# Attention with memory, leaky MLP and bilinear MLP on one core: the first batch's scores with tokens on partitions, the first chunk of w_out loaded by column halves, the last product in two column parts

## The chip, the cores and the metric

The kernel runs as one launch on one core of a Trainium2 chip. The metric is the device time of the launch in microseconds; the kernel before was timed three times. TensorE (PE) multiplies, VectorE (DVE) and ScalarE (ACT) convert, reduce and copy, SyncE (SP) issues every transfer, GpSimd (POOL) does almost nothing here. Each engine carries out its instructions strictly in the order in which they stand in the program.

## The reference

Three stages follow one another, all in float32 (the weights come as float64 words, which the kernel converts itself):

```python
a = exp(phi - max(phi, over m));  a = a / (sum(a, over m) + 1e-9)     # B=4, H=8, S=576, M=32
k_m = einsum('bhsm,bhsd->bhmd', a, k);  v_m = same with v             # D=64
s = q @ k_m^T / 8;  s = exp(s - max);  attn = s / (sum(s) + 1e-9)
x = (attn @ v_m) laid out as 2304 tokens x 512
h = x @ w_in                      # 512 -> 2048
y = maximum(0.01*h, h) @ w_out    # 2048 -> 512
out = ((y @ w_a) * (y @ w_b)) @ w_out2     # 512 -> 1536 -> 512
```

## The kernel before

**Stages.** For each batch `b` a head (`kv_part`, line 547; `sc_both`, line 653) loads phi, k and v, takes the exponentials of phi (ACT, line 537), turns them on PE (`ta`, `tz`, lines 584 and 587), copies them to SBUF (`en`, line 407), multiplies them with k and v (`km`, line 603: 20 float32 matmuls of two passes each), scales (`kvn`, line 613), turns the result (`kvt`, line 623) and copies it out as `kd` (keys) and `vm` (values). Scores (`sc`, line 667) come with the 32 memory slots on partitions and tokens along the row, 320 or 256 columns; DVE turns them in squares of 32 (line 688), and max, subtraction, ACT's exponential (line 699), sum, reciprocal and product (lines 697 to 707) run on 128 partitions; a second turn (line 711) gives `at`.

**The first MLP.** `w_in` and `w_out` are taken in four chunks `c` of 512 hidden columns, each in four pieces of 512 KB (`weight`, line 451). A piece is two ACT passes (`high` and `low`, lines 470 and 473) and four DVE passes (clamp, shift, join, add; lines 477 to 488); `w_out` is then split into two fp32r parts (a cast, line 407, and a subtraction, line 494). `vw` (line 750) multiplies `vm` into `w_in`, so that `h` (lines 803 and 821) is attention times `vw`. Batch 0 of chunk 0 uses plain float32 (`vwf`, `gf`, lines 803, 774 and 867); everything else three fp32r passes. Tokens go in eight pieces `n`: piece `x` = 0 of batch 0 has 320 columns, `x` = 1 has 256. Each of the four `h` of a piece is read by ACT (line 774), mostly twice: once to `g`, once to `t`.

**The second MLP.** Products with `w_a` and `w_b` by seven instead of eight sub-products (line 1092 and 1146), then `o` (line 1186), an add on DVE (line 1199), and two output transfers per 512 columns (line 1205).

**Order.** A planner (`Program`, lines 113 to 333) sets the order once, when the program is built. Each operation has a cost on the engines that may do it, a due time `late` (worked back from the main products' times, less a `slack`), and tiles that must find a free buffer in a room. At each moment every engine takes the ready operation that is due first. PSUM has eight banks: room "h" is three of them (for `h`), "y" two, "x" three (for `ta`, `tz`, `km`, `kvt`, `sc`, `vw`). SP's transfers are planned the same way and land one after another. After some tiles of the head, `idle` (line 430) puts four PE transpositions that compute nothing (line 434), and `warm` (line 424) puts 38 of them at the start.

Of the kernel before, what the change touches and what calls it, by code (L numbers as in the profile page):

```python
# [53 lines left out]
FULL = (0,)  # L54
TURN = 0.15
FILL = 4
WARM = 38
SEVEN = 8
LEAD = 37
SLACK = {'phi0': 72.94, ('kv0', 0): -15.48, ('kv0', 1): -17.72, 'kvr0': -10.62, ('q0', 0): 4.66, ('q0', 1): 32.32, ('win0', 0): 0.75, ('win0', 1): 103.86, ('wout0', 0): 20.54, ('wout0', 1): -39.84, 'win': -23.08, 'wout': 22.71, 'wa': -4.25, 'wb': -26.57, 'wout2': -2.14, ('sc', 0, 0): 57.16, ('sc', 0, 1): -2.31, ('sc', 1, 0): 13.24, ('sc', 1, 1): 6.37, ('sc', 2, 0): 23.27, ('sc', 2, 1): 24.61, ('vw', 0, 0): 85.06, ('vw', 0, 1): -56.75, ('vw', 0, 2): 18.69, ('vw', 1, 0): 5.23, ('vw', 1, 1): 100.39, ('vw', 1, 2): 9.67}  # L60
START = 15.05
BIAS = 0.52
POOL_BIAS = 9.26
LAT, LAT_SAME, LAT_DMA = 0.503, 0.134, 3.8
OVER = {'DMA': 0.0, 'PE': 0.0, 'ACT': 0.1, 'DVE': 0.019, 'POOL': 0.0}
BLOCKED = 2.31
DMA_RATE = 355000.0
SPARE = {'DMA': 1.27, 'PE': 1.0, 'ACT': 1.03, 'DVE': 1.03, 'POOL': 0.96}

# [38 lines left out]
class Program:  # L108
# [13 lines left out]
    def op(self, eng, cost, fn, r=(), w=(), tiles=(), pos=None, ahead=60.0, keep=0, slack=0.0, soon=False):  # L122
# [213 lines left out]
def tile_mem_attention__leaky_mlp__bilinear_mlp(  # L336
# [93 lines left out]
    def idle(tile, get, token):  # L430
# [20 lines left out]
    def weight(kind, c, k, after=()):  # L451
# [73 lines left out]
    def phi_stats(b, gs, phi, st):  # L525

        nmx, es, er = ([(n, b % 2, g) for g in gs] for n in ("nmx", "es", "er"))
        part = slice(gs[0], gs[-1] + 1)
        e = [("e", b, g) for g in gs]
        op(  # L530
            "DVE", c_dve(S * len(gs)), lambda T: nc.vector.tensor_reduce(st[0][:, part], T[phi], axis=AX.X, op=ALU.max, negate=True),
            r=e, w=nmx, tiles=[phi],
        )
# [12 lines left out]

    def kv_part(b, g):
# [49 lines left out]

        def k_m(T):
            for t in range(5):
                n = P if t < 4 else 64  # L600
                src = T[kvt[t // 2]][:, t % 2, :] if t < 4 else T[rest][:, g, :]
                for h in range(4):
                    nc.tensor.matmul(  # L603
                        T[km][h * M:(h + 1) * M, :], T[en][0:n, t, h * M:(h + 1) * M], src[:, h * P:(h + 1) * P],
                        start=(t == 0), stop=(t == 4),
                    )

        op("PE", 1.5, k_m, r=[(en, 0), (en, 1), *kvt, rest], w=[km], tiles=[en, *kvt, rest, km])

# [31 lines left out]
    def q_load(b, g):
# [5 lines left out]
        for x in range(2):  # L647
# [3 lines left out]
            op("DMA", c_dma(P * n * 8), lambda T, q=q, cols=cols: nc.sync.dma_start(T[q], qT[b, g, :, :, cols]), w=[q], tiles=[q], slack=SLACK["q0", x])  # L651

    def sc_both(b, x):

        cols = piece(2 * b + x)
        n = cols.stop - cols.start
# [14 lines left out]

        op("PE", 4 * n / 2.4e3 + TURN, s_sc, r=[*qs, *(("kd", b % 2, g) for g in range(2))], w=scs, tiles=[*qs, *scs])
        NM = n // 32
# [58 lines left out]
    def vw_unit(c, b, x, n):  # L732
# [12 lines left out]
        def prod(T):  # L745
# [6 lines left out]
        op(  # L752
            "PE", TURN + 4 * n / 2.4e3, prod, r=[("a", k[1:]) for k in ws] + [("vm", b, g) for g in range(2)], w=os, tiles=[*os, *ws],
            ahead=15.0,
        )
        slack = SLACK["vw", min(c, 1), b - b % 2 if c else min(b, 2)]
        for i, o in enumerate(os):
            if whole(c, b):
                op(copy_by(n, True), 0, lambda T, e, i=i, o=o: copy(e, T[fk][:, i, cols], T[o]), r=[o], w=[(fk, i, x)], tiles=[o, fk], slack=slack)
                if b == 0:  # L760
                    idle(fk, lambda t, i=i: t[:, i, x * n:x * n + P], (fk, i, x))
                continue
# [27 lines left out]
    def h_unit(c, n, f, pos):  # L790
# [5 lines left out]
        if whole(c, b):  # L796
# [48 lines left out]
    def y_unit(c, k, e, pos, part=None):  # L845
# [12 lines left out]
        gs = [g_of(c, k, f) for f in range(4)]  # L858
        ws = [("wout", c, f) for f in range(4)]
        n, fine = ns[0], whole(c, ns[0] // 2)  # L860
        if fine:
            gf, cvs = ("gf", n), [("cv", "wout", c, f) for f in range(4)]

        def prod(T):
            for f, (g, j) in enumerate(gs):
                if fine:
                    nc.tensor.matmul(T[o], T[cvs[f]][:, 0, es].bitcast(F32), T[gf][:, f, :], start=f == 0, stop=f == 3)  # L867
                    continue
                w = T["wout", c, f]
# [297 lines left out]

    def o_unit(s, c, l, e, pos):


        size = NB2 if l < 2 else B * LEFT
        o = ("o", s, c, l, e)
        ps_ = [(("p", s, x, l), 0) if l < 2 else (("pl", c // 2), x % 2) for x in (c, c + 1)]
        ws = [("wout2", x, s) for x in (c, c + 1)]
# [4 lines left out]
        else:  # L1179
            tile_of(acc, "slot", [2, size] if l < 2 else [4, size])  # L1180
        es = slice(e * P, (e + 1) * P)

        def prod(T):
            for x, ((g, at), w) in enumerate(zip(ps_, ws)):
                for k, (u, v) in enumerate(PASSES):
                    nc.tensor.matmul(  # L1186
                        T[o], T[w][:, u, es], T[g][:, at, v, :], start=(x == 0 and k == 0), stop=(x == 1 and k == 2)
                    )
# [8 lines left out]
        else:  # L1197
            op(
                "DVE", c_dve(size), lambda T: nc.vector.tensor_tensor(T[acc][:, i, :], T[o], T[acc][:, i, :], op=ALU.add),  # L1199
                r=[o], w=[ka], tiles=[o, acc],  # L1200
            )
        if c == NC2 - 2:
            for at, w, to in places_of(s, l):
                op(
                    "DMA", c_dma(P * w * 4), lambda T, at=at, w=w, to=to: nc.sync.dma_start(out[:, e, to:to + w], T[acc][:, i, at:at + w]),
                    r=[ka], tiles=[acc], ahead=1e12,
                )
# [136 lines left out]
    for c in range(NC1):  # L1344
# [101 lines left out]
```

## Time and profile before

| | |
|---|---|
| three runs | 788.04, 787.47, 786.38 us; median 787.47 |
| profiled execution | 786.36 us, of which the span is 784.6 us |
| PE busy | 773.4 us (99%) |
| weight loads (PEld) | 663.4 us (85%) |
| DVE busy | 607.2 us (77%) |
| ACT busy | 379.1 us (48%) |
| DMA | 149.99 MB, mean 191 GB/s |

Busy shares are means over the span. The page's 40 slices give PE 7 and 8 tenths in the first two, 9 tenths in all but the last; the granted TensorE clock is at 9 tenths or more in every slice.

### The profile page before, as it was taken

The page shows a single profiled execution, that of the slowest core. Times are in us where ns is not written, and L with a number is a line of the kernel's source. Part 1 is how long each engine was busy: PE and PEld are TensorE (multiplying, and loading weights), DVE is VectorE, ACT ScalarE, POOL GpSimd, SP SyncE. Part 2 cuts the span into 40 slices and gives each one's busy share as a digit, 9 for nine tenths or more (in the row PEclk, how much of TensorE's full clock was granted, in tenths as well). Part 3 has the DMA queues.
Part 4 walks back from the last instruction along what each step waited for, and adds up shares of the span by engine and source line. Part 5 has one row for each costly group of instructions (what it writes and reads, how often), then busy time and mean ns, then how long its engine had stood idle before and what let it go on. Part 6 is the DMA issues. An engine that isn't in the chain of part 4 may idle for free.

```text
span 784.6 us, 12658 instructions
## 1 busy us (share of the span) xinstructions
PE 773.4 (99%) x4822; PEld 663.4 (85%) x4822; DVE 607.2 (77%) x1149; ACT 379.1 (48%) x817; POOL 0.7 (0%) x6
## 2 busy tenths in 40 slices
PE   7899999999999999999999999999999999999997
PEld 6567898989898988998888888888888888888886
DVE  5888988868888865686745899998995667898865
ACT  5767777747465635453445454445332254223210
POOL 0000000000000000000000000000000000000000
PEclk9999999999999999999999999999999999999999
DMA  9993331573247300035867547475488586978503
GB/s 321 384 323 140 99 90 61 192 264 103 82 174 266 124 1 1 1 115 206 293 247 267 185 160 273 161 239 190 164 322 346 178 275 209 354 250 280 179 19 108
DMA packets 56557, 149.99 MB, mean 191 GB/s; under 512 B 7216, under 2 KB 22576, under 8 KB 56496
## 3 DMA queue, kind: packets, MB, share of 16 engines
q1 hardware_dynamic: 56496, 149.18, 54.5%
q8 instruction: 38, 0.62, 0.3%
q14 instruction: 23, 0.19, 0.1%
HBM read 103.55 MB, written 45.61 MB: 190 GB/s over the span
## 4 chain that ended last, share of the span: by engine, by line
PE 95%; DMA 2%; DVE 1%; SPq 0%; ACT 0%; issue 0%
PE y L871 24%; PE abx L1092 17%; PE o L1186 13%; PE h L821 13%; PE abz L1092 8%; PE os L1301 5%; PE aby L1092 4%; PE b L1146 2%; PE a L1146 2%; PE y L867 2%; PE vw L750 2%; DMA kv<-in_kv_dram 1%; DMA phi<-in_phiT_dram 1%; PE h L803 1%; PE km L603 1%; PE sc L667 0%
## 5 line engine op out<-in xcount | busy, mean ns | idle before, releaser
L871 PE MATMUL y<-g,wout 128*128 128x320 f32 (+2 forms) x1104 | 197.2, 333 | 0.0
L871 PEld LDWEIGHTS y<-g,wout 128*128 128x128 f32 x1104 | 175.6, 188 | 16.7 <-issue 2.1
L1092 PE MATMUL abx<-yb_T,wo 128*128 128x512 f32 x432 | 109.7, 389 | 0.0
L1103 ACT COPY t<-abx 128x512 f32<-128x512 f32 x72 | 42.3, 587 | 122.7 <-PE abx L1092 117.6
L1092 PEld LDWEIGHTS abx<-yb_T,wo 128*128 128x128 f32 x432 | 80.6, 188 | 16.4
L1186 PE MATMUL o<-p,wout 128*128 128x512 f32 x384 | 93.6, 389 | 0.0
L1186 PEld LDWEIGHTS o<-p,wout 128*128 128x128 f32 x384 | 71.9, 188 | 15.2 <-DVE osum L1199 0.4
L774 ACT ACTIVATE g<-h 128x256 fp32r<-128x256 f32 (+1 forms) x120 | 49.7, 414 | 52.9 <-PE h L821 50.8
L821 PE MATMUL h<-ahi,vwh 128*128 128x256 f32 (+1 forms) x240 | 72.7, 303 | 0.0
L821 PE MATMUL h<-ahi,vwl 128*128 128x256 f32 (+1 forms) x240 | 71.0, 296 | 0.0
L821 PE MATMUL h<-alo,vwh 128*128 128x256 f32 (+1 forms) x240 | 71.0, 296 | 0.0
L890 DVE TENSOR_TENSOR acc<-y,acc 128x320 f32<-128x320 f32 (+1 forms) x72 | 40.1, 557 | 36.6 <-PE y L871 35.7
L837 DVE TENSOR_TENSOR g<-t,g 128x256 fp32r<-128x256 f32 (+1 forms) x120 | 53.7, 453 | 15.4 <-ACT t L774 14.4
L821 PEld LDWEIGHTS h<-ahi,vwh 128*128 128x128 f32 x240 | 45.4, 189 | 10.2 <-issue 3.6
L774 ACT ACTIVATE t<-h 128x256 f32<-128x256 f32 (+1 forms) x120 | 49.5, 413 | 0.0
L821 PEld LDWEIGHTS h<-alo,vwh 128*128 128x128 f32 x240 | 45.4, 189 | 0.2
L821 PEld LDWEIGHTS h<-ahi,vwl 128*128 128x128 f32 x240 | 45.5, 190 | 0.0
L1100 DVE TENSOR_TENSOR t<-abz,t 128x512 f32<-128x512 f32 x48 | 33.0, 688 | 13.2 <-PE abz L1092 7.6
L1199 DVE TENSOR_TENSOR oacc<-o,oacc 128x512 f32<-128x512 f32 x40 | 27.6, 690 | 16.7 <-PE o L1186 16.2
L1092 PE MATMUL abx<-yb_B,wo 128*128 128x512 f32 x144 | 36.9, 391 | 0.0
L1092 PE MATMUL aby<-yb_B,wo 128*128 128x512 f32 x144 | 36.7, 390 | 0.0
L407 ACT CAST p<-t 128x512 fp32r<-128x512 f32 x32 | 19.9, 621 | 34.7 <-DVE t L1124 22.7
(289 smaller groups left out, 1276.1 us busy)
## 6 DMA issues: line engine op xcount, KB each, us to landing
k_wo<-wo SPq DMA_DIRECT2D x32, 512.0 KB, 4.4
wo<-k_wo SPq DMA_DIRECT2D x32, 512.0 KB, 4.9
raw_wout<-in_w_out_dram SPq DMA_DIRECT2D x24, 512.0 KB, 5.5
raw_win<-in_w_in_dram SPq DMA_DIRECT2D x16, 512.0 KB, 5.2
kv<-in_kv_dram SPq DMA_DIRECT2D x16, 512.0 KB, 10.4
k_yb_T<-yb_T SPq DMA_DIRECT2D x8, 512.0 KB, 5.9
raw_wa<-in_w_a_dram SPq DMA_DIRECT2D x8, 512.0 KB, 4.5
raw_wb<-in_w_b_dram SPq DMA_DIRECT2D x8, 512.0 KB, 5.4
```

The lines of the kernel that those rows point to most:

```text
L774: nc.scalar.activation(dst, src, AF.Prelu, alpha=0.01)
L821: nc.tensor.matmul(T[o], T[w[u]][:, k, fs], T[a[v]][:, k, cols], start=(k == 0 and i == 0), stop=(k == 1 and i == 2))
L837: lambda T, e: engines[e].tensor_tensor(T[g][:, i, 1, to], T[t], T[g][:, i, 0, to].bitcast(F32), op=ALU.subtract),
L871: nc.tensor.matmul(T[o], w[:, u, es], T[g][:, j, v, at:at + m], start=(f == 0 and p == 0), stop=(f == 3 and p == 2))
L890: "DVE", c_dve(m), lambda T: nc.vector.tensor_tensor(T[acc][:, i, :], T[o], T[acc][:, i, :], op=ALU.add),
L1092: nc.tensor.matmul(T[o], T[w][:, which, u, k * P:(k + 1) * P], T[ys[v]][:, k, :], start=first and k == 0 and x == 0, stop=k == 1 and x == ...
L1100: op("DVE", 0.69, lambda T: nc.vector.tensor_tensor(T[to], T[o], T[x], op=ALU.add), r=[o, x], w=[to], tiles=[o, x, to])
L1103: op("ACT", 0.59, lambda T: nc.scalar.copy(T[t], T[X]), r=[X], w=[t], tiles=[X, t])
L1146: nc.tensor.matmul(T[o], T[w][:, k // 2, u, k % 2 * P:(k % 2 + 1) * P], T[ys[v]][:, k, :], start=(k == 0 and x == 0), stop=(k == 3 and x = ...
L1186: nc.tensor.matmul(T[o], T[w][:, u, es], T[g][:, at, v, :], start=(x == 0 and k == 0), stop=(x == 1 and k == 2))
L1199: "DVE", c_dve(size), lambda T: nc.vector.tensor_tensor(T[acc][:, i, :], T[o], T[acc][:, i, :], op=ALU.add),
L1301: nc.tensor.matmul(T[o], lhs(T, u), T[g][:, v, :], start=k == 0, stop=k == 2)
```

## The change

Five things are changed, and the planner's numbers with them.

Scores of batch 0 come with tokens on partitions (`sc_tokens`). The query block of 128 tokens is the stationary operand, 32 columns of `kd` move; two blocks for the 256 columns of `x` = 1, three (one overlapping) for the 320 of `x` = 0. Max and subtraction read PSUM directly, no 32-square turns are made, and PE turns the finished weights back (`atp`), from where ACT copies them to `at`. Batches 1 to 3 keep `sc_both`. Evictions of `kd` and `vm` of batch 0 are separate for the two halves of the partitions, and `km` of batch 0 is given in three parts, the remainder `kvr` first.

```diff
+    def sc_tokens(b, x):
...
+                        nc.tensor.matmul(
+                            T[scs[i]][:, t, k * M:(k + 1) * M], T[qs[g]][half, j, c0:c0 + P], kd[b % 2][half, k, :], start=True, stop=True,
+                        )
...
+                "DVE", c_dve(w), lambda T, o=o, here=here: nc.vector.tensor_reduce(here, rows(T[o]), axis=AX.X, op=ALU.max),
...
+                "DVE", c_dve(w), lambda T, i=i, o=o, here=here: nc.vector.tensor_tensor(rows(T[sm][:, i]), rows(T[o]), wide(here, NM), op=ALU.subtract),
...
+        op("ACT", c_act(2 * w), lambda T: nc.scalar.activation(flat(T), flat(T), AF.Exp, scale=1.0 / float(D) ** 0.5), w=toks, tiles=[sm])
...
+                    nc.tensor.transpose(T[o][:, c0:c0 + P], T[sm][:, i, t, :], ident)
...
+        if b == 0:
+            sc_tokens(b, x)
+            return
```

The first chunk of `w_out` is loaded as the first chunk of `w_in` was: two row tiles by 256 columns a piece. Piece `x` = 1 of batch 0 goes through the first chunk before `x` = 0.

```diff
+        "wout": lambda c, k: w_out[c * FC + k * P:c * FC + (k + 1) * P, :] if c else
+        w_out[2 * (k % 2) * P:2 * (k % 2 + 1) * P, k // 2 * 256:(k // 2 + 1) * 256].rearrange("(j p) f -> p j f", p=P),
...
+FIRST = (1, 0, *range(2, NPIECE))
...
-        for n in range(NPIECE):
+        for n in (range(NPIECE) if c else FIRST):
```

The idle transpositions after two of the four `w_in` pieces, after `en` of batch 1 and after `vwf` are left out (twelve groups of four become four), `WARM` goes from 38 to 41. The last product, of 512 columns, is made as 320 and 192, each with its own add and transfer.

```diff
-        if kind == "win" and c == 0:
+        if kind == "win" and c == 0 and k > 1:
             idle(cv, lambda t: t[:, 0, 0:P].bitcast(F32), a)
...
+                        last = s == 1 and c == NC2 - 1 and l == 1 and e == 3
+                        for cols in [p[:2] for p in places_of(s, l)] if last else [None]:
+                            queue.append(lambda pos, s=s, c=c, l=l, e=e, cols=cols: o_unit(s, c - 1, l, e, pos, cols))
```

The planner's constants are new, and a table of 226 numbers is added to the slack of single operations:

```diff
-LEAD = 37
+LEAD = 75
...
-        o.slack, o.soon = slack, soon
+        o.slack, o.soon = slack + NUDGE.get(o.seq, 0.0), soon
```

So the order moves on all engines. SP now issues `w_in` pieces 2 and 3, phi, the remainder, the four k-v pieces of batch 0, and then `w_in` pieces 0 and 1; before, pieces 0 and 1 came ahead of the remainder and the k-v pieces. Three places follow.

On PE, around the first `h` of chunk 0. Before (`km`, `kvt` are batch 1's; `h_0_0` is piece 0):

```order
L603 MATMUL km_0_429<-kv_0_0_297,en_0_389 32x128 x8
L603 MATMUL km_0_429<-kv_0_1_306,en_0_389 32x128 x8
L603 MATMUL km_0_429<-kvr_385,en_0_389 32x128 x4
L603 MATMUL km_1_454<-kv_1_0_331,en_1_406 32x128 x8
L603 MATMUL km_1_454<-kv_1_1_358,en_1_406 32x128 x8
L603 MATMUL km_1_454<-kvr_385,en_1_406 32x128 x4
L623 MATMUL kvt_0_485<-ident,kvn_0_481 128x128 x2
L803 MATMUL h_0_0_490<-at_0_479,vwf_318 128x320 x2
```

After (`h_1_0` is piece 1; lines have moved):

```order
L741 MATMUL atp_0_1_426<-ident,sm_1_362 128x128 x2
L741 MATMUL atp_1_1_431<-ident,sm_1_362 128x128 x2
L905 MATMUL h_1_0_445<-at_1_438,vwf_313 128x256 x2
L608 MATMUL km_0_449<-kv_0_0_289,en_0_409 32x128 x8
L608 MATMUL km_0_449<-kv_0_1_310,en_0_409 32x128 x8
L608 MATMUL km_0_449<-kvr_384,en_0_409 32x128 x4
L741 MATMUL atp_0_0_476<-ident,sm_0_407 128x128 x3
L741 MATMUL atp_1_0_480<-ident,sm_0_407 128x128 x3
L608 MATMUL km_1_486<-kv_1_0_336,en_1_429 32x128 x8
L608 MATMUL km_1_486<-kv_1_1_351,en_1_429 32x128 x8
L608 MATMUL km_1_486<-kvr_384,en_1_429 32x128 x4
L905 MATMUL h_1_1_513<-at_1_438,vwf_313 128x256 x2
```

Both `km` of batch 1, one `kvt` and the turns of piece 0 have moved from ahead of the first `h` to behind it.

On ACT, from the reading of piece 0's `h` (`gf`) to the copies of batch 2's turns (`en`). Before, the same copies, behind the last `gf`:

```order
L774 ACTIVATE gf_555<-h_1_3_565 128x256
L407 CAST ahi_568<-at_1_498 128x2x256
L407 COPY acc_0_609<-y_0_0_590 128x320
L537 ACTIVATE phi_533,es_78<-phi_533,nmx_77 128x576 x2
L407 COPY acc_0_609<-y_0_1_601 128x320
L699 ACTIVATE sm_0_595<-sm_0_595 128x512
L407 COPY en_0_643<-ta_0_617 128x512
L407 COPY en_1_645<-ta_1_627 128x512
L407 COPY en_0_643<-tz_0_624 64x128
```

After:

```order
L876 ACTIVATE gf_575<-h_0_1_571 128x320
L475 ACTIVATE cv_wout_2_585<-raw_wout_2_507 128x512
L542 ACTIVATE phi_472,es_78<-phi_472,nmx_77 128x576
L876 ACTIVATE gf_575<-h_0_2_579 128x320
L542 ACTIVATE phi_472,es_78<-phi_472,nmx_77 128x576
L475 ACTIVATE cv_wout_3_616<-raw_wout_3_516 128x512
L876 ACTIVATE gf_575<-h_0_3_603 128x320
L411 COPY en_0_623<-ta_0_609 128x512
L803 ACTIVATE sm_1_582<-sm_1_582 128x640
L411 COPY en_0_623<-tz_0_626 64x128
```

The exponentials of batch 2 and two `w_out` pieces now stand between the `gf`, and the exponential of 640 columns has come between the copies of `ta_0` and `tz_0`. On PE the three turns `ta_0`, `tz_0`, `ta_1` follow `h_0_3` at once, where before two `y` (eight matmul rows) stood ahead of them.

On ACT, at the end of chunk 0 (`h_7`, the last piece, 320 columns). Before:

```order
L774 ACTIVATE g_4_3_1444<-h_6_3_1507 128x256
L774 ACTIVATE t_6_3_1541<-h_6_3_1507 128x256
L774 ACTIVATE g_5_0_1544<-h_7_0_1518 128x320
L774 ACTIVATE t_7_0_1554<-h_7_0_1518 128x320
L473 ACTIVATE cv_win_0_1557<-raw_win_0_1450 128x512
L774 ACTIVATE g_5_0_1544<-h_7_1_1533 128x320
L774 ACTIVATE t_7_1_1568<-h_7_1_1533 128x320
```

After:

```order
L876 ACTIVATE g_4_3_1425<-h_6_3_1525 128x256
L876 ACTIVATE t_6_3_1548<-h_6_3_1525 128x256
L411 CAST wout_0_1557<-cv_wout_0_1174 128x512
L876 ACTIVATE g_5_0_1560<-h_7_0_1537 128x320
L411 CAST wout_1_1570<-cv_wout_1_1203 128x512
L411 CAST wout_2_1573<-cv_wout_2_1226 128x512
L411 CAST wout_3_1576<-cv_wout_3_1253 128x512
L876 ACTIVATE t_7_0_1579<-h_7_0_1537 128x320
```

Four casts of `w_out` have come between the two readings of `h_7_0`; on PE the four `h_7` stand one right behind the other, in three banks.

## Rows read from the trace of the kernel before

**Rows 1.** Windows: busy time of each engine, granted clock, DMA share, GB/s.

```profile
43.00:100.00 57.00, 57.00 (x608) 44.80 (x609) 48.95 (x101) 39.85 (x109) 0.00 (x0) 1.00 0.51 172
```

**Rows 2.** Timeline of PE, start: start, length, what, [idle before, releaser].

```profile
1.35 6.67 PE L426 MATMUL warm<-ident 128*128 128x128 f32 x38 [1.35 <-POOL ident masks.py:199]
...
23.29 0.77 PE L667 MATMUL sc<-q,kd 64*32 64x320 f32 x16
23.99 1.09 PE L434 MATMUL warm<-ident,vwf 128*128 128x128 f32 x8
...
33.01 3.50 PE L803 MATMUL h<-at,vwf 128*128 128x320 f32 x12 [0.33 <-DVE at L711]
...
39.46 2.86 PE L803 MATMUL h<-at,vwf 128*128 128x256 f32 x12 [0.78 <-ACT gf L774]
```

**Rows 3.** Timeline of weight loads: first use of the last k-v piece of batch 0.

```profile
17.97 0.38 PEld L603 LDWEIGHTS km<-kv,en 128*32 128x32 f32 x16 [0.23 <-DMA kv<-in_kv_dram]
```

**Rows 4.** Lines of ACT, shapes apart, 0 to 100 us: count, busy, mean ns, idle before.

```profile
L537 ACT ACTIVATE phi<-phi,nmx 128x576 f32<-128x576 f32 x8 | 6.1, 770 | 1.7 <-DVE nmx L531 1.7
L470 ACT ACTIVATE cv_wout<-raw_wout 128x512 f32<-128x512 f32 x8 | 5.3, 683 | 1.5 <-DMA raw_wout<-in_w_out_dram 1.4
L407 ACT COPY en<-ta 128x512 f32<-128x512 f32 x8 | 4.5, 588 | 0.7 <-PE ta L584 0.7
...
L774 ACT ACTIVATE t<-h 128x320 f32<-128x320 f32 x8 | 3.5, 438 | 0.0
...
L699 ACT ACTIVATE sm<-sm 128x640 f32<-128x640 f32 x4 | 2.9, 735 | 0.0
...
L407 ACT COPY kd<-kvt 64x64 f32<-64x64 f32 x12 | 2.4, 204 | 0.5 <-DVE vm L409 0.4
L407 ACT COPY en<-tz 64x128 f32<-64x128 f32 x8 | 2.0, 260 | 0.0
...
L407 ACT CAST wout<-cv_wout 128x512 fp32r<-128x512 f32 x3 | 1.9, 626 | 0.0
...
L407 ACT COPY vwf<-vw 128x256 f32<-128x256 f32 x4 | 1.3, 376 | 1.2 <-PE vw L750 1.2
```

**Rows 5.** Lines of DVE, same view and stretch.

```profile
L766 DVE TENSOR_TENSOR vwl<-vw,vwh 128x256 fp32r<-128x256 f32 x12 | 4.6, 409 | 0.9 <-ACT vwh L407 0.8
L531 DVE TENSOR_REDUCE nmx<-phi 128x2 f32<-128x1152 f32 x3 | 4.0, 1324 | 1.9 <-DMA phi<-in_phiT_dram 1.9
...
L485 DVE SCALAR_TENSOR_TENSOR cv_win<-raw_win,cv_win 128x512 int32<-128x512 int32 x4 | 2.8, 690 | 0.1
...
L477 DVE TENSOR_SCALAR cv_win<-cv_win 128x512 f32<-128x512 f32 x4 | 1.7, 421 | 5.5 <-ACT cv_win L470 5.5
```

**Rows 6.** Timeline of DVE: two instructions in a row.

```profile
30.34 0.82 DVE L707 TENSOR_TENSOR sm<-sm,sr 128x640 f32<-128x640 f32 x1
31.08 0.68 DVE L702 TENSOR_REDUCE sr<-sm 128x16 f32<-128x512 f32 x1
```

**Rows 7.** The chain of waits, 30 to 100 us: start, length, what.

```profile
47.41 0.44 PE ta L584 x4
...
69.61 1.36 PE km L603 x40
70.97 1.08 PE h L821 x6
...
78.23 0.22 PE kvt L623 x2
78.45 1.43 PE y L871 x12
...
93.61 0.88 PE h L821 x6
```

**Rows 8.** Timeline of the end: adds on DVE, output transfers' issues.

```profile
771.89 10.32 SPq L1205 DMA_DIRECT2D out_dram<-osum  x12
...
780.69 0.69 DVE L1199 TENSOR_TENSOR osum<-o,osum 128x512 f32<-128x512 f32 x1 [0.67 <-PE o L1186]
```

More of the change, by code (lines that the diff above doesn't have):

```diff
@@ L62 @@
+START = 30.38
 BIAS = 0.52
[L63 to L66, printed above, removed]
+POOL_BIAS = 19.78
+LAT, LAT_SAME, LAT_DMA = 0.424, 0.288, 6.42
+OVER = {'DMA': 0.0, 'PE': 0.0, 'ACT': 0.1, 'DVE': 0.057, 'POOL': 0.0}
+BLOCKED = 5.85
 DMA_RATE = 355000.0
-SPARE = {'DMA': 1.27, 'PE': 1.0, 'ACT': 1.03, 'DVE': 1.03, 'POOL': 0.96}
+SPARE = {'DMA': 1.17, 'PE': 1.0, 'ACT': 1.03, 'DVE': 1.03, 'POOL': 1.4}
 def c_dve(n):
@@ L531, in phi_stats @@
             "DVE", c_dve(S * len(gs)), lambda T: nc.vector.tensor_reduce(st[0][:, part], T[phi], axis=AX.X, op=ALU.max, negate=True),
[L532 removed]
+            r=e, w=nmx, tiles=[phi], slack=SLACK["nmx"] if b else 0.0,
         )
@@ L596, in kv_part, with k_m @@
         tile_of(km, "x", [P])
-        def k_m(T):
-            for t in range(5):
+        def k_m(T, ts, first, last):
+            for t in ts:
                 n = P if t < 4 else 64
-                src = T[kvt[t // 2]][:, t % 2, :] if t < 4 else T[rest][:, g, :]
+                src = T[kvt[t // 2]][:, t % 2, :] if t < 4 else T[rest][:, g, 0:512]
                 for h in range(4):
@@ L604, in k_m @@
                         T[km][h * M:(h + 1) * M, :], T[en][0:n, t, h * M:(h + 1) * M], src[:, h * P:(h + 1) * P],
-                        start=(t == 0), stop=(t == 4),
+                        start=first and t == ts[0], stop=last and t == ts[-1], skip_group_check=True,
                     )
-        op("PE", 1.5, k_m, r=[(en, 0), (en, 1), *kvt, rest], w=[km], tiles=[en, *kvt, rest, km])
+        parts = KM_FIRST[g] if b == 0 else ((0, 1, 2, 3, 4),)
+        for i, ts in enumerate(parts):
+            need = list(dict.fromkeys(kvt[t // 2] if t < 4 else rest for t in ts))
+            op(
+                "PE", 0.29 * len(ts) + 0.05, lambda T, i=i, ts=ts: k_m(T, ts, i == 0, i == len(parts) - 1),
+                r=[(en, 0), *([(en, 1)] if 4 in ts else []), *need], w=[km], tiles=[en, *need, km],
+            )
         def norm(T, e):
@@ L670, in s_sc @@
                         )
-        op("PE", 4 * n / 2.4e3 + TURN, s_sc, r=[*qs, *(("kd", b % 2, g) for g in range(2))], w=scs, tiles=[*qs, *scs])
+        op("PE", 4 * n / 2.4e3 + TURN, s_sc, r=[*qs, *(("kd", b % 2, g, i) for g in range(2) for i in range(2))], w=scs, tiles=[*qs, *scs])
         NM = n // 32
@@ L752, in vw_unit @@
         op(
-            "PE", TURN + 4 * n / 2.4e3, prod, r=[("a", k[1:]) for k in ws] + [("vm", b, g) for g in range(2)], w=os, tiles=[*os, *ws],
+            "PE", TURN + 4 * n / 2.4e3, prod, r=[("a", k[1:]) for k in ws] + [("vm", b, g, i) for g in range(2) for i in range(2)], w=os, tiles=[*os, *ws],
             ahead=15.0,
@@ L1186, in prod @@
                     nc.tensor.matmul(
-                        T[o], T[w][:, u, es], T[g][:, at, v, :], start=(x == 0 and k == 0), stop=(x == 1 and k == 2)
+                        T[o], T[w][:, u, es], T[g][:, at, v, here], start=(x == 0 and k == 0), stop=(x == 1 and k == 2)
                     )
@@ L1198, in o_unit @@
             op(
-                "DVE", c_dve(size), lambda T: nc.vector.tensor_tensor(T[acc][:, i, :], T[o], T[acc][:, i, :], op=ALU.add),
-                r=[o], w=[ka], tiles=[o, acc],
+                "DVE", c_dve(size), lambda T: nc.vector.tensor_tensor(T[acc][:, i, here], T[o], T[acc][:, i, here], op=ALU.add),
+                r=[o, ka], w=[(ka, base) if cols else ka], tiles=[o, acc],
             )
```

126 lines of the change are left out of this document (100 added, 26 removed).

## The prediction

> **What bounds the kernel now.** I read the busy shares first, then windows, then the chain of waits, then each engine's timeline around the places where the order changes. PE is busy 773.4 of 784.6 us, and from 43 to 100 us it is busy 57.00 of 57.00 at a granted clock of 1.00 [rows 1]; the slices say the same up to the last. So behind 43 us the kernel takes what its matmuls take, and an edit moves the time in three ways only: by when the first main product starts, by matmuls that move from ahead of it (where PE waits for others) to behind it (where nothing hides them), and by waits that PE gets and hadn't. The first main product starts at 33.01, released by DVE's turn of the weights [rows 2]; there DVE and ACT are the bound, PE has so much room that it fills gaps with transpositions that compute nothing [rows 2]. One wait of PE lies behind it, 0.78 us at 39.46 for ACT [rows 2]. At the end the last add waits 0.67 for PE and takes 0.69, then come two output issues [rows 8].
>
> Prices on PE by starts in the chain: six fp32r products of 320 columns 0.88, twelve of 256 columns 1.43, so 0.147 and 0.12 each; 40 passes of a `km` 1.36; two turns 0.22 and four 0.44, so 0.11 each [rows 7].
>
> **First main product: -1.8.** The four first transfers aside, the k-v pieces of batch 0 now come before `w_in` pieces 0 and 1. The bytes ahead of and with piece 1 are those that before ended with the last k-v piece, which PE took up at 17.97 [rows 3]; so piece 1 lands near 17.95 and piece 0 one piece earlier, near 16.65 (512 KB at some 400 KB per us, the rate at which 4.9 MB came by 17.97, less the start). ACT then has, in order: `high` of piece 0, three small copies, `low`, four small copies, `high` of piece 1. That is 3 x 0.68 + 7 x 0.2 = 3.44 [rows 4], with 0.2 for waits: through at 20.3. DVE then has clamp and shift 2 x 0.42, join 0.69, two adds at 0.68 (as the 512-column rows), reduction and subtraction of 256 columns for `x` = 1 four times 0.41, batch 1's maximum 1.32, sum 0.68, two small ones some 0.4, and the same four for `x` = 0 at 384 columns, some 0.55 each, between 0.41 and 0.69 [rows 5, 6]: 9.2, less 0.08 of overlap at a dozen places (31.08 lies 0.08 before the end of 30.34 + 0.82 [rows 6]), so 8.3 and 28.6. ACT follows with the exponential of 768 columns (0.735 for 640 and a tenth more: 0.83), both `en` copies (0.26 + 0.59) and the two `at` copies (2 x 0.376) [rows 4], 2.4 or a little more: first product at 31.2, against 33.01. The scores' own products lie beside DVE's chain: before, 16 listed matmuls of 320 columns took 0.70 from 23.29 to 23.99 [rows 2], that is 0.044 each. The new ones have 128 columns of weights and 32 that move, a shape no row shows: from 0.044 (80 passes, 3.5 us) to the 0.11 that a turn of 128 by 128 takes (8.8 us); I take the low half, since 0.07 still fits beside DVE.
>
> **Work moved behind it: +3.6.** The two `km` of batch 1, one `kvt` and six turns of `x` = 0 stood ahead of the first `h` or didn't exist; now they stand behind: 2 x 1.36 + 0.22 + 6 x 0.11 = 3.6 [rows 7]. A full group behind `km` took 1.08 where it takes 0.88 elsewhere [rows 7]; one or two more such places: +0.3.
>
> **A wait at batch 2's turns: +1.9.** Two score tiles hold two of the three banks, so `tz_0` waits for the copy of `ta_0` on ACT. From the end of `h_0_1` ACT has three `gf` (3 x 0.44), two `high` (2 x 0.68), two exponentials (2 x 0.77, and some 0.1 each for the sums they hand over) and the copy 0.59: 5.0 by durations [rows 4], some 4.4 with seven overlaps like DVE's. PE has two `h` of 320 columns (3.50 less its tail for three, so 1.1 each [rows 2]), a score block 0.6 and a turn 0.44: 3.2. So 1.2. Behind that, `ta_1` waits for the copy of `tz_0`, which is queued behind the 640-column exponential, 0.735 [rows 4]: +0.7. Queued behind the turns on PE is the first `y`, and behind the copies on ACT the two `low` of `w_out`, which nothing needs for a while. Bounds: 0 (ACT is early at `gf`) and 3 (all by durations).
>
> **A wait at the last piece of chunk 0: +1.2.** `h_7_3` needs the bank of `h_7_0`, whose second reading is behind four casts. From the start of `h_7_0`: ACT is through with `h_6_3` and the first cast after about 1.3, then 0.44 + 3 x 0.626 + 0.44 = 2.76 by durations, 2.3 with overlaps [rows 4]: 3.6 to 4.1. PE gets to `h_7_3` after 3 x 0.88 = 2.64 [rows 7]. Bounds 0.9 and 1.5, and 0 if ACT were ahead.
>
> **What goes: -0.8 and -0.5.** The wait of 0.78 at 39.46 [rows 2] goes: with piece 1 first, `km`, turns and `kvt` lie between the `h`, and ACT has time for `gf`. Next late is the turn of batch 2, counted above. At the end, six products of 512 columns take 0.69 + 0.67 = 1.36 [rows 8]; in parts 6 x (0.147 + 0.12) = 1.60, +0.24, if 192 columns are no dearer than 256. The last add is then of 192 columns, about 0.34 (256 columns take 0.41 [rows 5]) instead of 0.69, and one issue instead of two follows: both end at 782.21, 0.83 behind the add's end at 781.38 [rows 8], so 0.4 each. -0.35 - 0.4 + 0.24 = -0.5.
>
> The halves of `w_out`'s first chunk cost the same passes on ACT and DVE and the same bytes: 0. Fewer idle turns: 0, they lay in gaps; their other effect is a rival.
>
> **Sum.** -1.8 + 3.6 + 0.3 + 1.9 + 1.2 - 0.8 - 0.5 = +3.9. On the profiled execution's 786.36 that is 790.3; the median of the runs is 1.11 above that execution, so 791.4. 0.2% (1.6 us) is about what a measurement can tell from no change; so slower.
>
> **Rivals.**
>
> Weight loads show (0.12). If each of the 80 score passes costs 0.11, PE needs 8.8 instead of 3.5 us ahead of the first product, 5.3 more; some 2 fit into gaps that the left-out idle turns leave there (eight groups at 0.5 [rows 2], half of them in this stretch), so +3.3: 794.7. For: PEld is busy 85% and the shape has all 128 columns. Against: halves of the partitions alternate, as in the old scores, which ran at 0.044. The Trainium skill, "TensorE: Matmul & The Clock Gate", section "LDWEIGHTS (loading the stationary operand)", says that a load's time goes with its columns and not its rows, columns / 1.2 in ns; by that the old scores' 32 columns told nothing of the new ones, and 80 loads would be an estimated 8.5 us in series, the same place as the upper bound. The same page under "The mechanism" lets a load overlap a running matmul only where the row groups differ, which halves it to about 4.3. No run here shows either yet.
>
> The clock falls (0.05). The 38 turns of the warm-up took 6.67 us [rows 2] where at 0.11 they take 4.2: 2.5 us for a renewed slow stretch. With the idle turns gone, PE has gaps from 18 to 31. Against it: before, the gap of 0.78 at 39.46 left it at 1.00 [rows 1, 2]. 793.9. The skill's same page, "Part 1: The HAM clock gate", says that the throttled state is the default and activity releases it; in the trace the clock stays granted through the head.
>
> ACT keeps up, the other side (0.12). All three waits hang on ACT or DVE. If ACT reads piece 1 at its landing (-2.35), DVE overlaps a little more (-0.4) and ACT is 2 us ahead at both later places, the first product is at 28.45 (-4.55), the waits are 0, and the sum is -4.55 + 3.6 + 0.3 - 0.8 - 0.5 = -1.95: 785.5. It turns faster from a first product at about 28.8. For: small copies can slip in while piece 0 is on its way. Against: their sources (`kvt`) come only behind the k-v pieces.
>
> It cancels (0.11). First product as forecast, no wait at the two places: -1.8 + 3.6 + 0.3 - 0.8 - 0.5 = +0.8, so 788.3. For: 0.12 and more of slack on ACT would do; against: both queues are written out in the order.
>
> **Chances.** Forecast 0.60, the rivals as given. Forecast, loads and clock are slower, but 0.02 of the forecast's spread is within 0.2%: slower 0.75, same 0.13, faster 0.12. The forecast's own range, with its waits' bounds (0 to 3, 0.9 to 1.5) and half of the loads: 789.3 to 794. For 8 in 10 the range goes to 795.5 above (loads) and to 786.6 below (the edge of the other side).
>
> **What would show it.** First `h` of chunk 0 at 31.2 (right), at 29 or below (other side), at 34 or above (loads). Score passes at 0.044 to 0.07 a product, or at 0.11. Between the first `h` and the second, `km` x40 twice and the turns. An idle of PE before `tz` and `ta` of batch 2, released by ACT's `en` copies, and one before the last `h` of chunk 0, released by ACT's `t`. Granted clock 1.00 from 6 us on. From there to the last add no other gap; the end 0.5 shorter. What makes it wrong: ACT more than 1 us earlier at either place, or a wait that the order hides from me in the second MLP, where the planner's new numbers reorder DVE's sums.

## The result and the profile after

The changed kernel takes 794.57 us in the median (four runs, 794.11 to 795.06) against 787.21 for the kernel before beside it: ratio 1.0094, 95% interval 1.0076 to 1.0111, so 7.4 us slower. The forecast was 791.4 in a range of 786.6 to 795.5 for 8 in 10, of which 789.3 to 794 was the forecast's own. The profiled execution took 794.23, its span is 792.4, 7.8 longer.

Three lines of the page after, PE's share, the slices of PE and those of the granted clock:

```profile
PE 779.8 (98%) x4857; PEld 669.2 (84%) x4857; DVE 609.2 (77%) x1161; ACT 375.3 (47%) x808; POOL 0.7 (0%) x6
...
PE   7999999999999999999999999999999999999998
...
PEclk9699999999999999999999999999999999999999
```

The second slice of the clock is new: 6 tenths, while PE is at 9 tenths in it. Windows of the changed kernel show where (columns as in [rows 1]):

```profile
16.00:18.00 2.00, 0.66 (x4) 0.20 (x2) 1.48 (x4) 1.53 (x5) 0.00 (x0) 1.00 1.08 359
18.00:19.00 1.00, 0.40 (x9) 0.31 (x16) 0.78 (x2) 0.93 (x4) 0.00 (x0) 1.00 1.07 364
...
20.00:21.00 1.00, 1.00 (x22) 1.00 (x20) 1.00 (x3) 0.97 (x3) 0.00 (x0) 1.00 0.99 392
21.00:22.00 1.00, 1.00 (x18) 1.00 (x18) 0.97 (x2) 0.17 (x1) 0.00 (x0) 0.74 1.04 414
22.00:23.00 1.00, 1.00 (x14) 1.00 (x12) 0.97 (x3) 0.00 (x0) 0.00 (x0) 0.50 1.03 411
...
34.00:35.00 1.00, 1.00 (x24) 0.92 (x28) 0.00 (x0) 0.38 (x1) 0.00 (x0) 0.50 1.05 413
35.00:36.00 1.00, 1.00 (x25) 0.60 (x18) 0.00 (x0) 0.03 (x1) 0.00 (x0) 0.94 1.03 392
```

PE is idle for about two thirds of 16 to 19 us, then busy 1.00 of 1.00, and yet the granted clock goes from 1.00 (2.4 GHz) to 0.50 (1.2 GHz) at 21.5 and stays there until 35.1. All four runs lost it: their mean granted clock is 0.989 to 0.991. PE's timeline of the same stretch, where [rows 2] had the old scores and the first `h`:

```profile
18.60 0.89 PE L854 MATMUL vw<-cv_win,vm 64*32 64x256 f32 x16 [1.30 <-ACT vm L411]
19.42 5.39 PE L685 MATMUL sct<-kd,q 64*128 64x32 f32 x64
24.74 1.10 PE L854 MATMUL vw<-cv_win,vm 64*32 64x256 f32 x16
25.77 1.92 PE L685 MATMUL sct<-kd,q 64*128 64x32 f32 x16
...
31.89 2.07 PE L905 MATMUL h<-at,vwf 128*128 128x256 f32 x4 [0.30 <-ACT at L411]
33.89 1.66 PE L608 MATMUL km<-kv,en 128*32 128x128 f32 x32
...
36.64 1.08 PE L608 MATMUL km<-kv,en 128*32 128x128 f32 x32
...
38.00 1.13 PE L905 MATMUL h<-at,vwf 128*128 128x256 f32 x4
...
48.79 0.30 PE L592 MATMUL tz<-ident,phi 128*64 128x128 f32 x1 [0.92 <-ACT en L411]
49.57 0.66 PE L589 MATMUL ta<-ident,phi 128*128 128x128 f32 x4 [0.48 <-ACT en L411]
```

The first `h` starts at 31.89 (33.01 before), runs at half clock (2.07 against 1.13 for the same shape at 38.00), and so does most of the first `km` behind it (1.66 against 1.08). At 48.79 and 49.57 stand the two waits at batch 2's turns, 1.40 together; the wait of 0.78 before the `h` at 39.46 [rows 2] is gone. All waits of PE from 60 us on, longest sum first:

```profile
PE os L1410 <- ACT osum L411: 1.3, 1, 1.3
PE h L923 <- ACT t L876: 0.8, 1, 0.8
```

The second is the one foreseen at `h_7_3`. The first was not. ACT's timeline at 648 us, and the chain's piece that it hangs on:

```profile
648.44 0.59 ACT L411 COPY osum<-os 128x512 f32<-128x512 f32 x1
652.62 0.62 ACT L411 CAST pb_T<-pT 128x512 fp32r<-128x512 f32 x1 [3.60 <-DMA out_dram<-oacc]
653.15 0.58 ACT L411 COPY osum<-os 128x512 f32<-128x512 f32 x1
```

```profile
647.12 5.40 DMA out_dram<-oacc
```

A cast that needs the buffer of an output still on its way (the releaser of `pb_T` is the transfer out of `oacc`) holds ACT for 3.60 us; behind it in ACT's queue stands the copy that frees PE's bank. DVE's adds at the end, where [rows 8] had one of 512 columns last:

```profile
787.56 0.69 DVE L1306 TENSOR_TENSOR osum<-o,osum 128x512 f32<-128x512 f32 x1 [0.67 <-PE o L1293]
...
788.44 0.49 DVE L1306 TENSOR_TENSOR osum<-o,osum 128x320 f32<-128x320 f32 x1 [0.18 <-PE o L1293]
789.26 0.36 DVE L1306 TENSOR_TENSOR osum<-o,osum 128x192 f32<-128x192 f32 x1 [0.33 <-PE o L1293]
```

From the last add of 512 columns that is not the last product's to the end: 792.4 - 787.56 = 4.84. Before it was one add earlier than [rows 8], 784.6 - (780.69 - 1.36) = 5.27.

### The profile page after: what moved, and what is told of

The parts are those of the page before. It is cut to its first block, busy times and chain, and to the rows that moved or that the text cites. A ratio compares the mean times of both kernels' runs of the same rounds, so it can differ in the third digit from the quotient of the medians.

```text
span 792.4 us, 12746 instructions
## 1 busy us (share of the span) xinstructions
PE 779.8 (98%) x4857; PEld 669.2 (84%) x4857; DVE 609.2 (77%) x1161; ACT 375.3 (47%) x808; POOL 0.7 (0%) x6
## 4 chain that ended last, share of the span: by engine, by line
PE 95%; DMA 3%; ACT 2%; SPq 0%; issue 0%; DVE 0%; ACTq 0%
PE y L975 24%; PE abx L1196 16%; PE o L1293 13%; PE h L923 12%; PE abz L1196 8%; PE os L1410 4%; PE aby L1196 4%; PE vw L854 2%; PE b L1250 2%; PE a L1250 2%; PE y L971 2%; DMA raw_win<-in_w_in_dram 2%; PE km L608 1%; PE h L905 1%; PE sct L685 1%; DMA out_dram<-oacc 1%
## 5 line engine op out<-in xcount | busy, mean ns | idle before, releaser
L975 PE MATMUL y<-g,wout 128*128 128x320 f32 (+2 forms) x1104 | 200.2, 334 | 0.0
L1293 PE MATMUL o<-p,wout 128*128 128x512 f32 (+2 forms) x390 | 95.5, 387 | 0.0
L1196 PE MATMUL abz<-yb_B,wo 128*128 128x512 f32 x144 | 36.7, 390 | 0.0
```

The lines of the kernel that those rows point to most:

```text
L975: nc.tensor.matmul(T[o], w[:, u, here], T[g][:, j, v, at:at + m], start=(f == 0 and p == 0), stop=(f == 3 and p == 2))
L1196: nc.tensor.matmul(T[o], T[w][:, which, u, k * P:(k + 1) * P], T[ys[v]][:, k, :], start=first and k == 0 and x == 0, stop=k == 1 and x == ...
L1293: nc.tensor.matmul(T[o], T[w][:, u, es], T[g][:, at, v, here], start=(x == 0 and k == 0), stop=(x == 1 and k == 2))
```

## The experiments

Theory: the time is the sum that the prediction names, plus a clock that falls because PE has too little to do ahead of and among the new scores, plus one wait that an output transfer makes. Rivals: the score passes alone let the clock fall, whatever surrounds them; the missing idle turns do; ACT is short of time as a whole, so that waits only move. Each run stands beside runs of the kernel before on its chip; a difference is to these. No kernel but those so marked leaves any work out. Places in us are read from one profiled execution of each kernel; the same head has its first `h` at 33.01 in the kernel before and at 33.44 in before_tail, so a single place is known to about 0.4.

**gapfill.** Twelve turns that compute nothing, ahead of the first `vw` of batch 0.

```diff
+            if c == 0 and b == 0 and x == 1:
+                for _ in range(12):
+                    nc.tensor.transpose(T["warm",], ident, ident)
```

> The changed kernel with twelve turns of 128 by 128 that compute nothing put ahead of the first vw product, into the gap of 1.3 us in which PE waits for ACT before the first score product; nothing else moves. If the score products themselves let the clock fall (many loads, 32 columns that move), it falls to 0.50 all the same some 2 us after they begin, the first main product stays at 31.9 and the time at 794.6 (within 0.5). If the gaps ahead of them let it fall, the clock stays at 1.00, a pair of score passes stays at 0.112, the first product comes at 30.3 to 31, the products behind it run at full speed, and the time is 791.5 to 792.5.

Measured 792.84, +5.3 (1.0071, 1.0054 to 1.0087). Neither expectation whole: the clock still falls, but later and for a shorter time, the first `h` is at 30.51 and still at half clock. In all four executions the mean clock is above the changed kernel's (0.993 to 0.994 for 0.989 to 0.991).

```profile
20.00:25.00 5.00, 5.00 (x78) 4.12 (x78) 4.93 (x10) 2.00 (x6) 0.00 (x0) 0.76 1.03 410
25.00:30.00 5.00, 4.54 (x28) 3.79 (x26) 4.85 (x12) 3.96 (x10) 0.00 (x0) 0.50 1.03 283
30.00:35.00 5.00, 4.70 (x59) 3.08 (x62) 2.20 (x5) 2.59 (x8) 0.00 (x0) 0.72 1.02 391
```

**dense.** Four such turns ahead of each score block, none in the gap.

```diff
+            for _ in range(4):
+                nc.tensor.transpose(T["warm",], ident, ident)
             for g in range(2):
```

> The changed kernel with four turns of 128 by 128 that compute nothing ahead of each of the five blocks of 16 score passes; nothing else moves. If sparse score products let the clock fall, the turns among them keep it at 1.00: they cost 20 x 0.11 = 2.2 on PE but the 80 passes and all up to 35 us run at full speed, the first product comes at 31 to 32, the 1.6 us lost behind it come back: 792.3 to 793.3. If the clock falls for another reason, the turns run at half speed too, 4 us more ahead of the first product, and the time is 797 to 799.

Measured 800.40, +12.9 (1.0164, 1.0149 to 1.0179). My theory's number missed by 7, the rival's 797 to 799 by 1.4. The clock fell before the turns came:

```profile
15.00:20.00 5.00, 2.93 (x40) 1.24 (x37) 2.26 (x5) 3.33 (x11) 0.00 (x0) 0.82 1.08 375
20.00:25.00 5.00, 5.00 (x38) 4.28 (x36) 2.06 (x4) 1.24 (x4) 0.00 (x0) 0.50 1.03 408
```

```profile
18.00:18.50 0.50, 0.00 (x0) 0.00 (x0) 0.47 (x2) 0.47 (x2) 0.00 (x0) 0.75 1.06 358
```

```profile
18.68 1.33 PE L856 MATMUL vw<-cv_win,vm 64*32 64x256 f32 x16 [1.44 <-ACT vm L411]
```

It fell inside PE's gap of 1.44, ahead of the first score pass, so in this execution the scores were not what let it fall, though PE's order up to there is that of the changed kernel, where it fell at 21.5. It then stayed at 0.50 until 42.1, and the first `h` came at 39.7. Whether the scores let it fall whatever stands between them was still open.

**gapdense.** Both, and five turns ahead of the second `kvt` of batch 0: 37 in all.

> The changed kernel with 37 turns that compute nothing: 5 in the gap ahead of the second kvt of batch 0, 12 ahead of the first vw, 4 ahead of each of the five score blocks. If the clock falls because PE is idle or nearly so between 15 and 22 us, and turns alone among the scores came too late (the clock had fallen at 18.5, ahead of them), it now stays at 1.00: 80 passes at 0.056 and 20 turns end near 27, the first main product comes at 29.5 to 30.5, what follows runs at full speed, 790.5 to 792. If the score passes let it fall whatever stands between them, the turns run at half speed and the time is 796 to 800.

Measured 793.67, +6.7 (1.0076, 1.0062 to 1.0090). The clock is at 1.00 in every window of the head, with the same 80 score passes:

```profile
20.00:25.00 5.00, 5.00 (x66) 4.37 (x68) 4.32 (x10) 1.38 (x4) 0.00 (x0) 1.00 1.02 406
25.00:30.00 5.00, 4.34 (x60) 3.15 (x58) 3.91 (x9) 3.21 (x10) 0.00 (x0) 1.00 1.03 298
30.00:35.00 5.00, 4.18 (x59) 2.81 (x60) 3.75 (x8) 3.65 (x9) 0.00 (x0) 1.00 1.03 395
```

```profile
21.46 1.08 PE L689 MATMUL sct<-kd,q 64*128 64x32 f32 x16
22.47 0.66 PE L684 MATMUL warm<-ident 128*128 128x128 f32 x4
...
31.74 1.13 PE L912 MATMUL h<-at,vwf 128*128 128x256 f32 x4 [0.52 <-ACT at L411]
```

So the scores do not let the clock fall whatever surrounds them. The first `h` is now 1.13 long; but the turns cost so much on PE that it starts at 31.74, later than expected, and the time missed its window by 1.7.

**sctcheap.** Two score products per block instead of eight (the other six of each block are left out).

```diff
-            for g in range(2):
-                for j in range(2):
-                    for i in range(2):
...
+            for i in range(2):
+                half = slice(i * 64, i * 64 + 64)
+                nc.tensor.matmul(
+                    T[scs[i]][:, t, :], T[qs[0]][half, 0, c0:c0 + P], kd[b % 2][half].rearrange("p k m -> p (k m)"), start=True, stop=True,
+                )
```

> The changed kernel with two score products per block of 128 tokens instead of eight: the first head pair's query against all 128 key columns, so that the scores of batch 0 are other numbers; queue orders are the same. 20 passes remain of 80. If the many sparse score passes make the head late and let the clock fall, the clock stays at 1.00 from 6 us on, PE no longer stands on the chain ahead of the first main product, which comes at 28.5 to 30.5 (DVE's chain), the 1.6 us lost behind it come back, and the time is 789.5 to 791. If gaps and missing idle turns are what lets the clock fall, it still falls, and the time is 792 to 793.5.

Measured 792.95, +5.6 (1.0064, 1.0048 to 1.0079): the rival's number. With a quarter of the passes, and PE idle for 1.18, 0.81 and 1.35 between 17 and 26, the mean clock is 0.991 as in the changed kernel (0.993 in the three other executions). Fewer sparse passes alone do not hold it.

**cheapfill.** The same with 53 turns that compute nothing in the gaps.

> The changed kernel with two score products per block instead of eight (other numbers for batch 0's scores) and 53 turns that compute nothing, in PE's gaps and ahead of each block and of batch 1's turns. PE is then dense and has little work that counts. If the gaps are what lets the clock fall, it stays at 1.00, the first main product shows the bare chain of DVE and ACT, at 28.5 to 29.5 (the prediction worked out 31.2 for that chain), and the time is 788.5 to 790.5. If it still falls, 792 to 793.5.

Measured 790.34, +3.4 (1.0040, 1.0026 to 1.0054). Clock at 1.00; the first `h` shows the chain of DVE and ACT without PE:

```profile
20.00:25.00 5.00, 5.00 (x54) 3.32 (x52) 4.84 (x10) 2.00 (x6) 0.00 (x0) 1.00 1.03 409
```

```profile
29.03 0.66 PE L745 MATMUL atp<-ident,sm 128*128 128x128 f32 x4 [0.30 <-DVE sm L738]
30.21 1.13 PE L912 MATMUL h<-at,vwf 128*128 128x256 f32 x4 [0.52 <-ACT at L411]
```

30.21 is above the 28.5 to 29.5 expected and 1.0 below the 31.2 of the prediction. What holds the changed kernel's first `h` up until 31.89 can be read beside it. The same DVE instruction, the maximum of the last scores, comes at 26.50 here, right behind the one before it; in the changed kernel DVE waits 1.27 for PE's last score block, and ACT then 0.28 for a turn at half clock. Here, then in the changed kernel:

```profile
26.50 0.95 DVE L719 TENSOR_REDUCE mx_t<-sct 128x12 f32<-128x384 f32 x2
```

```profile
27.72 1.02 DVE L715 TENSOR_REDUCE mx_t<-sct 128x12 f32<-128x384 f32 x2 [1.27 <-PE sct L685]
```

```profile
30.83 0.26 ACT L411 COPY en<-tz 64x128 f32<-64x128 f32 x1 [0.28 <-PE tz L592]
```

An estimate for the changed kernel at full clock: five blocks at 1.01 and the `vw` between them at 0.59, both from gapdense's starts, would end at 19.42 + 5.05 + 0.59 = 25.1, before DVE asks for them at 26.4.

**fewfill.** The kernel before with eight of its twelve groups of idle turns left out, order the same.

```diff
-            for _ in range(FILL):
+            gone = tile[0] == "vwf" or tile[:2] == ("en", 1) or tile[0] == "cv" and tile[3] < 2
+            for _ in range(0 if gone else FILL):
```

> The kernel before with the same idle turns left out as in the change (eight of twelve groups), its order otherwise word for word. If missing idle turns let the clock fall, the granted clock drops between 20 and 33 us here too and the time rises by 1 to 3 us, to 788.5 to 790. If the new score products are the cause, the clock stays at 1.00 from 6 us on and the time stays at 787.2 (within 0.4).

Measured 788.57, +1.05 (1.0017, 1.0007 to 1.0028). The idle turns do carry the clock in the kernel before:

```profile
25.00:30.00 5.00, 3.36 (x56) 2.02 (x56) 4.90 (x11) 3.96 (x10) 0.00 (x0) 1.00 1.03 307
30.00:35.00 5.00, 4.04 (x53) 2.67 (x54) 4.74 (x11) 2.04 (x5) 0.00 (x0) 0.66 1.03 407
```

It falls for 3.4 us here, 13.7 in the changed kernel. The ten executions on record go from 787.28 at a mean clock of 0.998 to 790.89 at 0.991. In the profiled one `kvr` also lands late, so that its first use is at 30.96 and not at 30.25, and the first `h` comes at 34.45; in before_tail, where it is as late and the clock stays up, the first `h` is at 33.44, so about 1.0 is the clock's.

**km_before, km_after.** 64 of the 80 passes of batch 1's `km` left out, in either kernel (the loop of the kernel before; in the changed kernel each part of batch 1's `km` is cut to its first tile).

```diff
-            for t in range(5):
+            for t in range(1 if b == 1 else 5):
```

> The kernel before with the same 64 passes left out, which there stand ahead of the first main product. If the place of the work is what matters, nothing is gained, 787.0 to 787.8, since DVE's chain sets the first product. If km is paid wherever it stands, 785.0 to 785.5.

> The changed kernel with only the first of five parts of batch 1's two km products: 64 of 80 passes, 64 x 0.034 = 2.2 us on PE, are left out, loads and all else stay. If work behind the first main product is paid in full, the time falls by 2.2 to 2.8 (part of them ran at half clock): 791.8 to 792.4. If other engines bound that stretch, it falls by less than 0.8.

Before: 788.30, +0.9 (1.0015, 1.0005 to 1.0024); nothing is gained, the first `h` is at 32.86 for 33.01, and with less work for PE the clock is at 0.50 from 33.0 to 36.4:

```profile
31.94 0.44 PE L623 MATMUL kvt<-ident,kvn 128*128 128x128 f32 x2 [2.99 <-ACT kvn L613]
32.86 3.84 PE L803 MATMUL h<-at,vwf 128*128 128x320 f32 x7 [0.49 <-DVE at L711]
```

After: 793.45, +6.1 (1.0081, 1.0065 to 1.0098), 1.3 less than the changed kernel. Behind the first `h` the sum of its starts' distances is 2.6 shorter in `km`, as expected; but the scores began 0.3 later (behind ACT), the clock fell at 20.8 for 21.5, and the first `h` came at 32.88 for 31.89. Both times miss their windows through the clock; the place of the work counts as forecast.

**waits, waits2.** ACT's order in the changed kernel, PE's the same; the first list is that of waits, the second that of waits2.

```diff
+MOVES = [(318, 129), (327, 318), (153, 118), (557, 473), (566, 557), (575, 566), (2468, 2497)]
...
+MOVES = [(548, 489), (557, 548), (566, 557), (575, 566), (2468, 2497)]
...
```

In a pair the first operation goes behind the second: in the first list two `high` of `w_out` and the exponential behind the copies of batch 2's turns, three casts behind `t_7_0`, the `pb_T` cast behind three `os` copies; in the second the four casts (and their subtractions on DVE) behind `h_7_3`.

> The changed kernel with nine instructions of ACT and one of DVE put later in their queues, PE's order unchanged: two high passes of w_out pieces and the 640-column exponential behind the copies of batch 2's turns, three w_out casts behind the second reading of h_7_0, and one pb_T cast, that waited 3.6 us for an output transfer, behind three copies of os. If the waits of PE are a matter of order, all four go (0.97 + 0.55 + 0.85 + 1.35 = 3.7) and the time is 790.6 to 791.4. If ACT or DVE lack the time, the waits come back within some us at the next place, and less than 1.5 is gained: 793.1 or more.

> The changed kernel with four w_out casts on ACT and their four subtractions on DVE put behind the last reading of h_7_3, and the pb_T cast behind three os copies; PE's order unchanged. If order alone makes these waits, PE has no idle left between 60 and 790 us (0.85 and 1.35 gone) and the time is 792.0 to 792.8, the clock's fall left as it is. If the casts are needed soon after, a wait of y for DVE of about 1 us comes back, as when three casts alone were moved, and 793 to 793.7 results.

Measured 794.11, +6.6 (1.0087, 1.0069 to 1.0104), and 799.85, +12.5 (1.0150, 1.0130 to 1.0170). The waits of PE from 60 us on, of `waits` and of `waits2`:

```profile
PE y L991 <- DVE g L955: 1.0, 1, 1.0
```

```profile
PE y L991 <- DVE g L955: 4.1, 1, 4.1
```

The `os` wait is gone in both. `h_7_3`'s is gone too, and comes back at the next `y`, larger the later the casts are: DVE's subtractions for them stand ahead of the split of `g`. In `waits2` DVE itself stands idle for the casts:

```profile
122.91 2.50 DVE L515 TENSOR_TENSOR wout<-cv_wout,wout 128x512 fp32r<-128x512 f32 x4 [4.69 <-ACT wout L427]
```

So there it is the order again, and not a lack of DVE's time: a queue held up by an instruction that waits. Whether another order would save the wait at `h_7_3` is not shown; these two don't. At the turns 1.40 became 0.68 + 0.35: most of it is the reading of `h_0_3` and the copy of `ta_0` one after the other (0.44 + 0.59), not the exponentials ahead of them. The time of `waits` does not price its waits: in the profiled execution (795.89) the clock was at 0.50 from 11.3 to 14.7 and again from 21.5 to 38.6, and the first `h` came at 34.75:

```profile
10.00:15.00 5.00, 4.81 (x46) 3.55 (x46) 1.41 (x6) 2.24 (x6) 0.00 (x0) 0.66 1.02 403
```

In `waits2` the 4.1 us without PE also let the clock fall:

```profile
120.00:125.00 5.00, 1.66 (x8) 1.02 (x6) 2.09 (x4) 2.88 (x7) 0.00 (x0) 0.88 0.00 0
125.00:130.00 5.00, 4.20 (x10) 3.33 (x11) 5.00 (x15) 0.59 (x1) 0.00 (x0) 0.50 0.68 207
```

**osfix.** gapdense with the `pb_T` cast alone moved.

> The kernel gapdense (37 idle turns, clock at 1.00) with one ACT instruction moved: the pb_T cast, which at 648 us held ACT up for an output transfer, goes behind the next three os copies. PE waited 1.5 there in gapdense, in the changed kernel 1.3. If that wait is the cast's place in ACT's queue, PE has no idle of more than 0.3 between 130 and 790 us and the time falls from 793.67 to 792.0 to 792.6. If the copies or PE then wait for something else at that place, it stays above 793.2.

Measured 791.92, +4.6 (1.0061, 1.0042 to 1.0080), against +6.7 for gapdense: 2.2 less. The two intervals overlap, so it is the trace that decides: the distances between the starts of `os` sum to 1.8 less, and PE has no gap left there:

```profile
130.00:785.00 655.00, 654.95 (x3673) 568.63 (x3672) 507.99 (x946) 286.61 (x588) 0.00 (x0) 1.00 0.54 187
```

**before_tail.** The kernel before with the last product in two parts.

> The kernel before with one part of the change alone, the last product in parts of 320 and 192 columns; all else word for word. From the last but one add to the end the changed kernel took 4.84 against 5.27, so 0.43 less is expected here too: 0.2 to 0.6 below the kernel before, at the edge of what five rounds tell. If the split costs more on PE than it saves at the end, 0 to +0.4.

Measured 787.42, +0.5 (1.0003, 0.9995 to 1.0012): no difference that can be told. In its own trace the end, from the same add on, takes 785.4 - 780.29 = 5.1 (5.27 before, 4.84 in the changed kernel), so the split alone shows less than half of the 0.43; what made the rest stays open. No version here beats the kernel before.

## Why the prediction was right, and where it was short

Direction and range were right, the forecast 3.2 too low. That the range held is in part luck: 794.57 lies outside the forecast's own 789.3 to 794, and inside the stated range only because its top was set for another mechanism, loads that show at full clock, which did not come. By its own steps, on the profiled executions (forecast 3.9 of them, measured 7.9):

| step | forecast | measured | from |
|---|---|---|---|
| first main product | -1.8 | -1.1 | 31.89 for 33.01 |
| work moved behind it | +3.6 | +3.5 | `km` 2.73, `atp` 0.80, at full clock |
| places behind narrow groups | +0.3 | +0.3 | `h`'s 1.19 less its wait |
| batch 2's turns | +1.9 | +1.8 | 1.40 idle, the rest beside it |
| `h_7_3` | +1.2 | +0.85 | 0.8 to 0.9 idle |
| old wait | -0.8 | -0.8 | gone |
| end | -0.5 | -0.4 | 4.84 for 5.27 |
| clock behind the first product | 0 | +1.5 | `h` 0.94, `km` 0.58 longer than at 1.00 (cheapfill) |
| wait at 652 us | 0 | +1.5 | 1.3 idle; 1.8 less in osfix |

These make 7.2; the other 0.7 lies in small distances of the float32 `h`, `y` and the second MLP and was not looked into. With the clock held and the wait at 652 us gone (osfix) the kernel is still 4.6 slower than the kernel before, so the sign does not rest on the two steps that the forecast put at 0.

**The first product** was mis-sized in two opposite ways. The chain of DVE and ACT, worked out as 31.2, ends at 30.21 when nothing else is in its way: in cheapfill DVE takes up piece 1 at 20.09 for 20.3, needs 8.3 as forecast, and ACT then 1.8 for 2.6. But PE, taken to be beside the chain, was on it: 64 passes in 5.39 us. At full clock the pairs of passes start 0.112 apart, 0.056 a pass, near the low end of the forecast's bounds (0.044 to 0.11). At half clock they start 0.2135 apart, 0.107 a pass. That loads of the two halves overlap agrees with the Trainium skill, "TensorE: Matmul & The Clock Gate", section "The mechanism": the 4.3 us that the prediction estimated from it for 80 passes is near 80 x 0.056 = 4.5. So loads did not show at full clock as that rival had them (0.11 a pass); its price per pass came only with the lower clock.

**The clock** was that other rival, at a chance of 0.05 and a price of 2.5, and it came in every run of the changed kernel. It was set too low because one gap of 0.78 in a dense stretch had left the clock up [rows 2]. That row said nothing of a head in which PE is idle for two thirds of 3 us, as from 16 to 19 here. fewfill and km_before show how near the edge the head stands: each takes work from PE, and each lost the clock for some microseconds; waits2 lost it at 124 us behind a wait of 4.1. Its price in the changed kernel is 1.5 behind the first product, and some 1.5 of the 1.7 between 30.21 and 31.89 ahead of it: the 1.27 and 0.28 for which DVE and ACT waited for PE at half clock (cheapfill, above). The first is shown; the second rests on the estimate that at full clock the scores end at 25.1, since no run has these scores, this filler and the full clock. gapfill, which only shortens the fall, gains 1.4 there.

**The wait at 652 us** was one of the two things that the prediction named as able to make it wrong, "a wait that the order hides from me in the second MLP"; it sought it in DVE's sums, and it lay in a cast on ACT. It was visible in principle: a cast into a buffer that an output transfer still reads, in an in-order queue ahead of the copy that frees a bank. I did not follow the buffers there.

**The other side** (ACT keeps up) failed as thought: `kvt` comes only behind the k-v pieces, and the first `h` did not come near 28.8. That the moved work is paid in full behind the first product and for nothing ahead of it is the step that carried the sign; the pair of `km` runs bears it out.

## What to carry to other kernels

Work that moves across the point from which the bounding engine has no gap changes price from nothing to all of it; count it first. Idle filler in a head is worth its turns when it holds the clock, so leaving it out is an edit with a price, and real work ahead of the point is such a filler too. It is not free where the engine that runs it is on the path: in dense the turns ran at half clock and the time rose by 5.5 against the changed kernel. When the order of a long program is made anew, look in every in-order queue for instructions that wait for a transfer of an old buffer ahead of one that the bounding engine needs.

## What the runs showed of the hardware that was not expected

The clock fell and stayed low while PE was busy without a gap by the trace: from 20 to 25 us of the changed kernel it is busy 5.00 of 5.00 while the clock goes from 1.00 to 0.50 (the windows above), and in dense it is 5.00 of 5.00 at 0.50 in the window shown. Four turns of 128 by 128 ahead of each score block went with a clock of 1.00 in gapdense, where other turns filled the gaps ahead as well, and with 0.50 in dense, where it had fallen before they came. It is not the same in every execution either: up to 18 us PE's order is the same in the changed kernel and in dense, and the clock fell at 21.5 in the one profile and at 18.25 in the other; ten executions of fewfill differ by 3.6 us in time and from 0.998 to 0.991 in mean clock.
